# Converting doubles to floats on the chip: one DVE operation less per weight tile, and a parametric ReLU for the absolute value

## The chip, the core and the metric

The kernel runs on one core of a Trainium2 chip. Its time is device microseconds, from start to end of one execution. The engines are TensorE (PE), VectorE (DVE), ScalarE (ACT), GpSimd (POOL) and SyncE (SP), which here issues the transfers.

## The reference, cut to what matters

Three layers follow each other: an attention over a local window plus block summaries, a feed-forward layer with SoLU and a layer norm, and a feed-forward layer with ELU. Cut to the mathematics:

```python
B, H, S, D = 2, 8, 768, 64
k_sum, v_sum = blocks_of_32(k).max(), blocks_of_32(v).mean()
s = concat(where(|i - j| < 16, q @ k.T / 8, -1e9), q @ k_sum.T / 8 + log(32))
x = softmax(s) @ concat(v, v_sum)                      # 1536 tokens x 512

h = x @ w_in                                           # w_in 512 x 1024
z = h * softmax(h)
h = (z - mean(z)) / sqrt(var(z) + 1e-6) * g_ln @ w_out # w_out 1024 x 512

h = h @ w_in2                                          # w_in2 512 x 2048
out = where(h > 0, h, exp(h) - 1) @ w_out2             # w_out2 2048 x 512
```

The four weight matrices arrive as doubles (64-bit floats); q, k and v as 32-bit floats. Converting the weights to 32-bit floats is part of the kernel's work.

## The kernel before, in words

**Products.** The products with weights (h, y_ps, o_ps and c in the profile) run on PE in three matmuls each (`mm3x`, lines 105 to 107): both operands are split into a rounded high half and the rest, and high x high, high x low and low x high are added up. ACT writes a high half (`split`, L136; L147 where the weight is scaled by g_ln), DVE the low half (`lo_of`, L102; L148). The products of the attention run in plain 32-bit floats.

**Attention.** 24 steps of 64 queries, two per block of 128 tokens. For each step PE makes scores (s_ps, L216), DVE adds the mask and finds the minimum (L222), ACT takes exponentials (L225), DVE sums and inverts (L227, L228), POOL normalises (L230), PE transposes (p_ps, L235), ACT copies (pT, L237), and per two steps PE multiplies with v (x_ps, L252). The result becomes xT in a high half (ACT, L136) and a low half (DVE, L102).

**First layer.** 12 token blocks: h (PE), maximum (DVE, L277), exponential (ACT, L279), product (DVE, L280), sum of squares (ACT, L281), a few small operations, normalisation (POOL, L287), transposes (PE, L297) whose copies are lnT (ACT L299, DVE L102), then y_ps.

**Second layer.** First 512 tokens plain: h, ELU (L590 to L592), o_ps. The other 1024 tokens use a Strassen-like scheme on w_in2 (c in the profile). The converted w_out2 is stored to memory (w4d, L373) and fetched again (w4r, w4l, L402).

**Conversion of weights.** A tile of 128x512 doubles is loaded as pairs of 32-bit words (L114) into space that the results y (or bits) take later. `to_f32` then makes floats. Before, ACT takes the absolute value of the high word, read as a float (L123); POOL clamps it between two constants (L126); DVE shifts left by three and masks (L127); DVE takes the two top bits of the high word and ORs them in (L128); DVE shifts the low word right by 29 and ORs it in (L132). The 48 calls are 8 for w_in, 8 for w_out, 16 for w_in2 and 16 for w_out2. They share three buffers (conv) in turn. L127 of a tile waits on POOL, POOL on ACT, ACT on the load.

**Order.** A scheduler sets the order on PE, DVE, ACT and POOL from the operations' dependences and its own estimate of how long each takes; so a different operation moves others as well. SP's order is as written up to line 579, and PE's from line 650 on (the Strassen-like part). Conversions called with `pin` keep their place in the written order on ACT.

Of the kernel before, what the change touches and what calls it, by code (L numbers as in the profile page):

```python
# [9 lines left out]
F32 = mybir.dt.float32  # L10
# [4 lines left out]
AF = mybir.ActivationFunctionType  # L15
ALU = mybir.AluOpType
# [27 lines left out]
def f32_of(bits):  # L44
    return struct.unpack("f", struct.pack("I", bits))[0]

F64_TINY, F64_HUGE = f32_of(0x38000000), f32_of(0x47F00000)


@with_exitstack
def tile_kernel(ctx: ExitStack, tc: tile.TileContext, qd, kT, v, w_in, w_out, g_ln, w_in2, w_out2,
                ident_d, mask_d, avg_d, out):
    nc = tc.nc
    scale = 1.0 / math.sqrt(D)
# [60 lines left out]
    def to_f32(bits, outs=None, pin=False):  # L117
        words = bits.rearrange("p k (f two) -> p k f two", two=2)
        low, high = words[:, :, :, 0], words[:, :, :, 1]
        a = conv_t[:, state["conv"] % 3]  # L120
        state["conv"] += 1
        x = a.bitcast(F32)
        first = nc.scalar.activation(x, high.bitcast(F32), AF.Abs)  # L123
        if pin:
            tc.keep_in_program_order(first)
        nc.gpsimd.tensor_scalar(x, x, F64_HUGE, F64_TINY, op0=ALU.min, op1=ALU.max)  # L126
        nc.vector.tensor_scalar(a, a, 3, 0x3FFFFFF8, op0=ALU.logical_shift_left, op1=ALU.bitwise_and)  # L127
        nc.vector.scalar_tensor_tensor(a, high, -0x40000000, a, op0=ALU.bitwise_and, op1=ALU.bitwise_or)  # L128
        to = a if outs is None else outs
        if outs is not None:  # L130
            low, a = (t.rearrange("p (h k) f -> p h (k f)", h=2) for t in (low, a))
        nc.vector.scalar_tensor_tensor(to, low, 29, a, op0=ALU.logical_shift_right, op1=ALU.bitwise_or)  # L132
        return x
# [5 lines left out]
    def convert(bits, src, hi, lo, g=None, pin=False):  # L139
        if src is not None:  # L140
            load_words(bits, src)
        hi, lo = (t if len(t.shape) == 3 else t.rearrange("p (k f) -> p k f", k=KD) for t in (hi, lo))
        x = to_f32(bits, pin=pin)
        if g is None:
            split(hi, lo, x)
        else:
            nc.scalar.activation(hi, x, AF.Copy, scale=g)  # L147
            nc.vector.scalar_tensor_tensor(lo, x, g, hi.bitcast(F32), op0=ALU.mult, op1=ALU.subtract)  # L148
# [203 lines left out]
    def convert_w3(f, b):  # L352
        if f % 2 == 0:
            home(f // 2)
        to_f32(b, base_of(f).bitcast(I32), pin=True)
# [428 lines left out]
```

## Time and profile before

| | before |
|---|---|
| median of 3 runs (lowest to highest), us | 487.64 (487.32 to 488.69) |
| the profiled execution: its own time, us | 486.94 |
| the profiled execution: span, first to last instruction, us | 485.1 |
| mean granted TensorE clock | 0.995 |
| PE, DVE, ACT, POOL busy, us | 466.6, 332.4, 285.3, 125.7 |

The span is what the rows below are measured in; 1.8 us of the execution's own time lie around it. A busy share is an average over stages with different limits, and a busy PE is not a PE at its peak. What ended a wait is inferred from semaphores.

### The profile page before, as it was taken

Reading aid. Unit: us, or ns where it says so; the run is one execution under the profiler, and the core shown is the slowest. Engines: PE = TensorE matmul, PEld = TensorE weight load, DVE = VectorE, ACT = ScalarE, POOL = GpSimd, SP = SyncE. Lnnn points to the kernel's source line nnn. Section 1 sums busy time; section 2 is a strip of 40 time slices with the busy share of each in tenths; the row PEclk is TensorE's granted clock in tenths of the full one; section 3 lists DMA queues with packets and bytes.
Section 4 is the critical chain, followed back from the end, with each engine's and each line's share of the span. In section 5 each row is a group of like instructions: output and inputs, shape, how many; then the busy total and the mean of one; then the engine's idle time right before and its main releaser. Section 6 shows DMA issues by size and latency. Waiting matters only on the chain.

```text
span 485.1 us, 7476 instructions
## 1 busy us (share of the span) xinstructions
PE 466.6 (96%) x2600; PEld 391.0 (81%) x2600; DVE 332.4 (69%) x748; ACT 285.3 (59%) x623; POOL 125.7 (26%) x200
## 2 busy tenths in 40 slices
PE   7879999799999999999999999999999999999996
PEld 3566788689997998899888888888888888888885
DVE  3789868997688477979899999457575565550000
ACT  1776687995577347654964767467676666660001
POOL 2795376586544322313212200000000000000000
PEclk9989999999999999999999999999999999999999
DMA  8994997263253513397579752651212212388112
GB/s 276 356 363 144 291 276 226 84 201 109 82 167 107 153 55 117 101 336 264 180 255 334 277 208 98 214 177 45 84 47 86 86 45 87 104 300 290 45 43 86
DMA packets 40117, 82.47 MB, mean 170 GB/s; under 512 B 9616, under 2 KB 18448, under 8 KB 40080
## 3 DMA queue, kind: packets, MB, share of 16 engines
q1 hardware_dynamic: 40080, 82.00, 51.5%
q8 instruction: 20, 0.33, 0.3%
q14 instruction: 17, 0.14, 0.1%
HBM read 70.46 MB, written 11.53 MB: 169 GB/s over the span
## 4 chain that ended last, share of the span: by engine, by line
PE 80%; DVE 11%; DMA 4%; ACT 2%; issue 2%; POOL 0%; SPq 0%; DVEq 0%; POOLq 0%
PE o_ps L105 9%; PE o_ps L106 9%; PE o_ps L107 9%; PE h L107 6%; PE h L105 6%; PE h L106 6%; PE c L105 5%; PE c L106 5%; PE c L107 5%; PE y_ps L105 4%; PE y_ps L107 4%; PE y_ps L106 4%; DMA q_bd<-in_qd 3%; PE s_ps L216 2%; PE vs_ps L186 2%
## 5 line engine op out<-in xcount | busy, mean ns | idle before, releaser
L126 POOL TENSOR_SCALAR conv<-conv 128x512 f32<-128x512 f32 x48 | 37.4, 780 | 87.9 <-ACT conv L123 84.0
L230 POOL TENSOR_SCALAR sm<-sm,st 128x120 f32<-128x120 f32 x96 | 49.9, 537 | 29.9 <-DVE st L228 11.2
L105 PE MATMUL o_ps<-w4r,g_hl 128*128 128x512 f32 x128 | 49.8, 389 | 0.0
L106 PE MATMUL o_ps<-w4r,g_hl 128*128 128x512 f32 x128 | 49.8, 389 | 0.0
L107 PE MATMUL o_ps<-w4r,g_hl 128*128 128x512 f32 x128 | 45.3, 389 | 0.0
L105 PE MATMUL y_ps<-lnT,w_out 128*128 128x384 f32 x128 | 43.6, 341 | 1.0 <-DVE lnT L102 1.0
L105 PE MATMUL h<-w_in,xT 128*128 128x512 f32 x96 | 39.9, 418 | 3.4 <-ACT xT L136 3.3
L106 PE MATMUL y_ps<-lnT,w_out 128*128 128x384 f32 x128 | 43.2, 337 | 0.0
L107 PE MATMUL y_ps<-lnT,w_out 128*128 128x384 f32 x128 | 42.9, 337 | 0.0
L225 ACT ACTIVATE sm<-sm,st 128x120 f32<-128x120 f32 x96 | 36.7, 388 | 5.5 <-DVE st L222 3.8
L107 PE MATMUL h<-w_in,xT 128*128 128x512 f32 x96 | 39.1, 409 | 0.7 <-DVE xT L102 0.7
L106 PE MATMUL h<-w_in,xT 128*128 128x512 f32 x96 | 38.8, 406 | 0.0
L619 DVE COPY y<-o_ps 128x512 f32<-128x512 f32 x5 | 3.5, 690 | 42.9 <-PE o_ps L107 42.9
L591 ACT ACTIVATE y<-y 128x512 f32<-128x512 f32 x48 | 30.1, 630 | 0.8
L621 ACT ACTIVATE y<-o_ps 128x512 f32<-128x512 f32 x6 | 3.6, 599 | 43.9 <-PE o_ps L107 43.9
L123 ACT ACTIVATE conv<-y 128x512 f32<-128x512 f32 x30 | 20.1, 673 | 14.8 <-DMA y<-in_w_in 12.7
L216 PE MATMUL s_ps<-kw,q_bd 128*128 128x120 f32 x192 | 25.6, 276 | 2.6 <-DMA q_bd<-in_qd 1.7
L106 PEld LDWEIGHTS o_ps<-w4r,g_hl 128*128 128x128 f32 x128 | 24.1, 188 | 5.0
L107 PEld LDWEIGHTS o_ps<-w4r,g_hl 128*128 128x128 f32 x128 | 24.0, 188 | 5.0
L105 PEld LDWEIGHTS o_ps<-w4r,g_hl 128*128 128x128 f32 x128 | 24.0, 188 | 5.0
L216 PEld LDWEIGHTS s_ps<-kw,q_bd 128*128 128x128 f32 x192 | 24.0, 191 | 5.0 <-POOL kw L98 1.9
L102 DVE TENSOR_TENSOR g_hl<-y,g_hl 128x512 fp32r<-128x512 f32 x32 | 21.9, 685 | 8.6 <-ACT g_hl L136 8.5
(149 smaller groups left out, 1273.4 us busy)
## 6 DMA issues: line engine op xcount, KB each, us to landing
w4r<-w4d SPq DMA_DIRECT2D x38, 512.0 KB, 3.6
y<-in_w_in SPq DMA_DIRECT2D x16, 512.0 KB, 6.0
w4d<-w3f SPq DMA_DIRECT2D x16, 512.0 KB, 3.0
y<-in_w_out SPq DMA_DIRECT2D x14, 512.0 KB, 5.1
q_bd<-in_qd SPq DMA_DIRECT2D x24, 256.0 KB, 6.3
bits<-in_w_out SPq DMA_DIRECT2D x10, 512.0 KB, 5.4
w4l<-w4d SPq DMA_DIRECT2D x10, 512.0 KB, 4.9
vw<-in_v SPq DMA_DIRECT2D x24, 192.0 KB, 5.3
```

Source lines behind the costliest of these rows:

```text
L102: nc.vector.tensor_tensor(out_, x, hi.bitcast(F32), op=ALU.subtract)
L105: nc.tensor.matmul(ps, lhsT=l[0][ls], rhs=r[0][rs], start=first, stop=False, skip_group_check=parts)
L106: nc.tensor.matmul(ps, lhsT=l[0][ls], rhs=r[1][rs], start=False, stop=False, skip_group_check=parts)
L107: nc.tensor.matmul(ps, lhsT=l[1][ls], rhs=r[0][rs], start=False, stop=last, skip_group_check=parts)
L123: first = nc.scalar.activation(x, high.bitcast(F32), AF.Abs)
L126: nc.gpsimd.tensor_scalar(x, x, F64_HUGE, F64_TINY, op0=ALU.min, op1=ALU.max)
L186: nc.tensor.matmul(pst, lhsT=avg[:, c0:c0 + 128], rhs=vt, start=i == 0, stop=i == S // 128 - 1)
L216: nc.tensor.matmul(sps[:, p, 0:KW], lhsT=q_bd[n][:, p, :], rhs=kw[:, p, :], start=True, stop=True)
L225: nc.scalar.activation(sm[:, p, :], sm[:, p, :], AF.Exp, bias=nm[:, p:p + 1], scale=-1.0, accum_out=ss[:, p:p + 1])
L230: nc.gpsimd.tensor_scalar(sm[:, p, :], sm[:, p, :], ri[:, p:p + 1], 1.0, op0=ALU.mult, op1=ALU.mult)
L591: nc.scalar.activation(m, m, AF.Exp, scale=-1.0)
L621: nc.scalar.activation(o, ops[t], AF.Copy)
```

## The change

The high word of a double, read as a 32-bit float, has the double's sign, then the upper 8 of its 11 exponent bits as exponent, and 3 exponent bits and 20 bits of the fraction as fraction. The changed kernel multiplies this float by 2^-112 on ACT, by a parametric ReLU that multiplies negative values by another 2^32. After that a positive value has a float exponent from 0 to 31, a negative one from 32 to 63: the bit of value 32 is the sign. POOL clamps both sides, and one shift left by three on DVE drops the three top bits and puts sign, exponent and fraction where the 32-bit float has them. L128 of the old kernel falls away, and the mask of L127.

```diff
-F64_TINY, F64_HUGE = f32_of(0x38000000), f32_of(0x47F00000)
+TO_F32, SIGN_TO_28 = 2.0 ** -112, 2.0 ** 32
+MOST, LEAST = f32_of(0x0FF00000), f32_of(0x9FF00000)
...
-        first = nc.scalar.activation(x, high.bitcast(F32), AF.Abs)
+        first = nc.scalar.activation(x, high.bitcast(F32), AF.Prelu, scale=TO_F32, alpha=SIGN_TO_28)
         if pin:
             tc.keep_in_program_order(first)
-        nc.gpsimd.tensor_scalar(x, x, F64_HUGE, F64_TINY, op0=ALU.min, op1=ALU.max)
-        nc.vector.tensor_scalar(a, a, 3, 0x3FFFFFF8, op0=ALU.logical_shift_left, op1=ALU.bitwise_and)
-        nc.vector.scalar_tensor_tensor(a, high, -0x40000000, a, op0=ALU.bitwise_and, op1=ALU.bitwise_or)
+        nc.gpsimd.tensor_scalar(x, x, MOST, LEAST, op0=ALU.min, op1=ALU.max)
+        nc.vector.tensor_scalar(a, a, 3, None, op0=ALU.logical_shift_left)
```

In the changed file lines 50 to 127 of the old one stand one lower (105 to 107 are 106 to 108, L123 is L124, L127 is L128); from L132 on the numbers are the same. DVE issues 48 instructions less, the other engines as many as before, in an order that is partly new.

DVE at the first conversions, before (y is the loaded tile, conv the converted one, w_in_90 the low half of w_in):

```order
L127 TENSOR_SCALAR conv<-conv 128x512
L128 SCALAR_TENSOR_TENSOR conv<-y_65,conv 128x512
L132 SCALAR_TENSOR_TENSOR conv<-y_65,conv 128x512
L227 TENSOR_SCALAR st<-st 128x4
L228 RECIPROCAL st<-st 128x4
L102 TENSOR_TENSOR w_in_90<-conv,w_in_89 128x512
```

and now:

```order
L128 TENSOR_SCALAR conv<-conv 128x512
L132 SCALAR_TENSOR_TENSOR conv<-y_65,conv 128x512
L227 TENSOR_SCALAR st<-st 128x4
L228 RECIPROCAL st<-st 128x4
L103 TENSOR_TENSOR w_in_90<-conv,w_in_89 128x512
```

The two-input operation between shift and last step is gone; the rest stands as it did.

ACT ahead of the first xT, before (sm are softmax tiles, w_in_89 the high half of w_in):

```order
L123 ACTIVATE conv<-y_66 128x512
L225 ACTIVATE sm,st<-sm,st 128x120 x4
L136 ACTIVATE w_in_89<-conv 128x512
L225 ACTIVATE sm,st<-sm,st 128x120
L136 ACTIVATE xT<-x_ps 128x512
```

and now:

```order
L124 ACTIVATE conv<-y_66 128x512
L136 ACTIVATE w_in_89<-conv 128x512
L225 ACTIVATE sm,st<-sm,st 128x120 x5
L136 ACTIVATE xT<-x_ps 128x512
```

The rounding of w_in now stands ahead of the exponentials that it followed.

PE from the scores near 55 us of the old profile on, before (s_ps scores, x_ps product with v, p_ps transposes):

```order
L216 MATMUL s_ps<-kw_117,q_bd 128x120 x4
L252 MATMUL x_ps<-pT,vw_122 64x64 x8
L252 MATMUL x_ps<-pT,vw_121 64x64 x8
L235 MATMUL p_ps<-ident,sm 120x128 x4
L216 MATMUL s_ps<-kw_118,q_bd 128x120 x4
L235 MATMUL p_ps<-ident,sm 120x128 x4
L105 MATMUL h<-w_in_89,xT 128x512
L106 MATMUL h<-w_in_90,xT 128x512
L216 MATMUL s_ps<-kw_119,q_bd 128x120 x4
```

and now, with the same scores first:

```order
L216 MATMUL s_ps<-kw_117,q_bd 128x120 x4
L252 MATMUL x_ps<-pT,vw_122 64x64 x8
L252 MATMUL x_ps<-pT,vw_121 64x64 x8
L107 MATMUL h<-w_in_90,xT 128x512
L108 MATMUL h<-w_in_89,xT 128x512
L235 MATMUL p_ps<-ident,sm 120x128 x4
L216 MATMUL s_ps<-kw_118,q_bd 128x120 x4
L107 MATMUL h<-w_in_90,xT 128x512
L108 MATMUL h<-w_in_89,xT 128x512
L235 MATMUL p_ps<-ident,sm 120x128 x4
L216 MATMUL s_ps<-kw_119,q_bd 128x120 x4
L252 MATMUL x_ps<-pT,vw_124 64x64 x8
```

Before, eighteen h matmuls follow the last row shown, then the product with v and the transposes for the first scores; now eight more of the product with v (vw_123) follow, and those transposes directly.

## Rows read from the trace of the kernel before

**Rows 1.** The page: engine totals, busy us, share of the span, instructions.

```profile
PE 466.6 (96%) x2600; PEld 391.0 (81%) x2600; DVE 332.4 (69%) x748; ACT 285.3 (59%) x623; POOL 125.7 (26%) x200
```

**Rows 2.** PE's waits by releaser, whole span: us in total, times, longest.

```profile
PE h L105 <- ACT xT L136: 3.3, 2, 2.1
PE p_ps L235 <- POOL sm L230: 2.3, 3, 1.4
PE p_ps L235 <- DVE lnT L102: 1.2, 1, 1.2
PE y_ps L105 <- DVE lnT L102: 1.0, 1, 1.0
PE s_ps L216 <- ACT pT L237: 0.9, 1, 0.9
PE h L107 <- DVE xT L102: 0.7, 1, 0.7
```

**Rows 3.** Timeline of PE: start us, us, line, operation, [idle before].

```profile
54.59 0.39 PE L107 MATMUL h<-w_in,xT 128*128 128x512 f32 x1
54.81 1.05 PE L216 MATMUL s_ps<-kw,q_bd 128*128 128x120 f32 x8
55.79 1.15 PE L252 MATMUL x_ps<-pT,vw 120*64 120x64 f32 x32
56.87 0.65 PE L235 MATMUL p_ps<-ident,sm 128*120 128x128 f32 x4
...
91.08 0.62 PE L235 MATMUL p_ps<-ident,sm 128*120 128x128 f32 x4 [1.25 <-DVE lnT L102]
...
204.34 0.45 PE L105 MATMUL y_ps<-lnT,w_out 128*128 128x384 f32 x1 [1.03 <-DVE lnT L102]
```

**Rows 4.** Windows: busy us per engine (instructions), TensorE clock, DMA share, GB/s.

```profile
25.00:50.00 25.00, 21.20 (x139) 15.34 (x139) 22.01 (x74) 17.54 (x57) 17.69 (x29) 0.93 0.76 252
28.00:34.00 6.00, 5.07 (x20) 3.88 (x21) 3.83 (x8) 3.69 (x11) 5.82 (x10) 0.72 1.03 335
184.00:204.50 20.50, 19.46 (x117) 17.70 (x116) 19.62 (x38) 15.47 (x27) 6.44 (x7) 1.00 0.29 98
```

**Rows 5.** Operations that write conv: duration ns min/median/max, first and last start.

```profile
L126 POOL TENSOR_SCALAR conv<-conv x48: 608/620/2412, 13.8 to 277.5; 128x512 f32<-128x512 f32 x48
L127 DVE TENSOR_SCALAR conv<-conv x48: 391/417/848, 15.5 to 280.7; 128x512 int32<-128x512 int32 x48
L123 ACT ACTIVATE conv<-y x30: 652/672/702, 13.0 to 211.5; 128x512 f32<-128x512 f32 x30
L128 DVE SCALAR_TENSOR_TENSOR conv<-y,conv x30: 676/693/1501, 15.9 to 213.5; 128x512 int32<-128x512 int32 x30
```

**Rows 6.** Timeline of DVE, three of its L128 operations.

```profile
23.91 0.97 DVE L128 SCALAR_TENSOR_TENSOR conv<-y,conv 128x512 int32<-128x512 int32 x1
...
40.72 0.73 DVE L128 SCALAR_TENSOR_TENSOR conv<-y,conv 128x512 int32<-128x512 int32 x1
...
87.71 0.69 DVE L128 SCALAR_TENSOR_TENSOR conv<-y,conv 128x512 int32<-128x512 int32 x1
```

**Rows 7.** Timeline of POOL, normalising softmax tiles (L230).

```profile
28.11 3.09 POOL L230 TENSOR_SCALAR sm<-sm,st 128x120 f32<-128x120 f32 x4
...
33.01 1.40 POOL L230 TENSOR_SCALAR sm<-sm,st 128x120 f32<-128x120 f32 x4
...
43.40 2.54 POOL L230 TENSOR_SCALAR sm<-sm,st 128x120 f32<-128x120 f32 x4 [1.47 <-DVE st L228]
...
62.30 1.40 POOL L230 TENSOR_SCALAR sm<-sm,st 128x120 f32<-128x120 f32 x4 [0.56 <-DVE st L228]
```

**Rows 8.** Window of the L128 operations alone: DVE busy us (instructions).

```profile
180.00:210.00 30.00, 2.73 (x4) 1.00 0.36 117
```

**Rows 9.** Groups by line and shape, on ACT: busy us, mean ns, idle before.

```profile
L591 ACT ACTIVATE y<-y 128x512 f32<-128x512 f32 x48 | 30.1, 630 | 0.8
L123 ACT ACT_TABLE_LOAD x1 | 1.3, 1283 | 0.7 <-PEq L776 0.7
```

## The prediction

> **What bounds the kernel now.** First the line of engine totals: TensorE (PE) is busy 96% of the span, VectorE (DVE) 69%, ScalarE (ACT) 59%, GpSimd (POOL) 26% [rows 1]. So a change that takes work from DVE alone can win only what PE loses by waiting. Second, PE's waits by releaser: the six groups that end on ACT, POOL or DVE add up to 3.3 + 2.3 + 1.2 + 1.0 + 0.9 + 0.7 = 9.4 us [rows 2], and the last of them ends at 204.34 us [rows 3]. Behind that, PE's own work sets the end, and what DVE saves there buys nothing. Third, the windows: from 25 to 50 us DVE is busy 22.01 of 25 us while PE has 3.8 us free; from 28 to 34 us the granted clock is 0.72, a mixture of the two levels 1.2 and 2.4 GHz, after PE had waited for its operands [rows 4]. At full clock these 6 us would be worth 0.28 x 6 = 1.7 us less. Waits and clock together bound any gain at 9.4 + 1.7 = 11.1 us.
>
> The profiled execution took 486.94 us, 0.70 under the median of the runs shown (487.64, from 487.32 to 488.69). The sum is made against 486.94 and then carried over to the median. About 0.3%, 1.5 us, is what a measurement of this kernel can tell from no change.
>
> **The change part by part.**
> *Removed:* one two-input DVE operation (L128) from each of 48 conversions. The 30 in the row have a median of 0.69 us [rows 5]; 48 x 0.69 = 33 us of DVE time. What of it lies on PE's path is taken place by place:
>
> (a) 26 to 30 us. PE waits 2.1 us for ACT's high half of xT and then 0.7 us for DVE's low half [rows 2]. An L128 of 0.97 us at 23.91 stands in DVE's queue ahead of the softmax pieces and the converted weights that ACT works off before that high half [rows 6]. The new order on ACT puts the rounding of these weights (L136) ahead of four exponentials that it stood behind, so ACT now waits for the conversion first, and the high half gains little, by estimate 0.2 us. The low half comes 0.97 us earlier in DVE's own queue, less about 0.3 us in which DVE then waits for ACT. I take 0.65 us for both waits together; bounds 0 and 2.8.
>
> (b) 45 to 46 us. POOL waited 1.47 us for DVE's reciprocal before it normalised four tiles from 43.40 [rows 7]; an L128 of 0.73 us at 40.72 is in that DVE queue [rows 6]. PE's two shorter waits on POOL are here, 2.3 - 1.4 = 0.9 us [rows 2]. I take 0.7; bounds 0 and 0.9.
>
> (c) 91 to 95 us. PE waits 1.25 us for DVE's half of lnT [rows 3], and right behind it 1.4 us on POOL [rows 2]; DVE's queue has an L128 of 0.69 us at 87.71 [rows 6]. The whole row moves up once, so 0.7; bounds 0 and 2.65.
>
> (d) 203 us. PE waits 1.03 us on DVE's lnT [rows 3]. DVE is busy 19.62 of the 20.5 us ahead [rows 4], and four L128 lie there, 2.73 us [rows 8]: more than the wait, so all of it goes, 1.0; bounds 0 and 1.03.
>
> The other waits (0.9 us for ACT's pT, 3.3 - 2.1 = 1.2 of those for ACT's xT) have no conversion just ahead of them: 0, at best 2.1.
>
> *Altered:* the first DVE operation (L127) loses its mask and keeps 128x512 integers in and out. No row shows a shift alone; its nearest bounds are 0.391, the quickest with the mask, and 0.69, that of the two-input operation. I take its own median, 0.417 [rows 5], since size, type and number of tensors stay. ACT's Abs becomes a parametric ReLU, 48 times. No row shows that function; the nearest bound it by 0.630, an exponential of this size [rows 9], and by 1.34, twice the Abs (a second pass). I take 0.672 as before [rows 5], for Abs and exponential, two different functions, are 0.04 us apart. POOL's clamp only has other constants: 0.620 as before, bounds its own 0.608 and 2.412 [rows 5].
>
> *Moved:* no instruction leaves its engine, but the order on each is made anew. SP's transfers are the same; where their order differs is the stage that fetches w_in2 and w_out2 and stores the converted w_out2. There PE waits for no transfer now: past 204.34 us no wait of PE is listed [rows 2, 3]. So 0, with a wait of PE for w4r as what would refute it. The 33 us of DVE time give weights earlier in that stage, but PE takes them no earlier: 0.
>
> Sum: 0.65 + 0.7 + 0.7 + 1.0 = 3.05 us; 486.94 - 3.05 = 483.89, on the median **484.6 us**.
>
> **The port of DVE and POOL.** Four normalisations of POOL took 3.09 us from 28.11 us, beside a full DVE queue, and 1.40 us from 33.01 [rows 7]. So DVE's operations also cost POOL time, which (b) and (c) leave out, because two other two-input operations stay in every conversion and would fall on the same POOL work. The Trainium skill, page "SBUF — State Buffer", section "SBUF: two separate sides", says that a DVE operation with two SBUF inputs and a GpSimd operation that reads SBUF exclude each other for a whole instruction; the trace agrees (3.09 against 1.40). If that rule decided, both of PE's waits on POOL would go whole, 0.2 us more in (b) and 1.4 more in (c): a sum of 4.65, or 483.0 us.
>
> **The rivals.**
> *More comes back.* Waits chain, and a PE that stalls less keeps its clock. For: the clock of 0.72 and POOL's 3.09 - 1.40 = 1.69 us [rows 4, 7]. Against: each place has a second releaser (ACT in (a), POOL in (c)). With (a) to (d) gone whole (2.8 + 0.9 + 2.65 + 1.0 = 7.35) and half of the clock's 1.7, it is 8.2 us, 479.4 us; with all 11.1 us, 476.5.
>
> *Hidden.* The releasers behind DVE take over: ACT in (a), whose work the change does not shorten, POOL in (b) and (c). Only (d) is won: 486.6 us. For: the longest wait ends on ACT, and 2.3 us on POOL [rows 2]. Against: both wait on DVE there.
>
> *Slower, by PE's new row.* Near 55 us PE issues scores (L216), and its transposes of the softmax of these very scores (L235) come with two more blocks of scores and twenty h matmuls in between. In the new order there are only four h matmuls between them. PE's own work from the one to the other is then 0.98 + 1.08 + 0.65 + 0.98 + 0.65 + 0.98 + 1.08 us, by the distances of starts and the whole duration of the transposes, and 4 x 0.22 for h [rows 3]: 7.3 us. The softmax of these scores took from 54.81 [rows 3] to the end of POOL's work at 63.70 [rows 7], 8.9 us. PE's queue is in order, so what a round takes over 7.3 us becomes a wait: 1.6 us. With three such rounds (the new order packs the stretch of (c) as tightly) it is 4.8 us, in place of the 0.9 for pT, and (c)'s 0.7 is lost: 3.05 - 0.7 - 3.9 = -1.55, or 489.2. It decides from rounds of about 8.9 us on, three times. Against: by then DVE has some six L128, 4 us, less behind it.
>
> *The function costs a table.* If the parametric ReLU lay in another table than the exponential, each of the 48 conversions, which stand among exponentials on ACT, would add two loads of 1.28 us [rows 9]: 123 us of ACT. ACT is free for 41% of the span [rows 1], so most is hidden; a tenth at the end gives 500 us. Against: the changed program holds one load, as the old one. A ReLU that is only slow, 1.34 us, adds 48 x 0.67 = 32 us; a tenth, 3.2 us, would cancel the sum. The Trainium skill, page "ScalarE: Activation LUTs", section "What ACT_TABLE_LOAD costs", gives a switch as 1283 ns and a drain, 2.66 us; the trace's one load agrees with the first figure, no run shows the second. By it the tenth would be 26 us, 513 us.
>
> **How the numbers follow.** The forecast (1.5 to 5 us won) 0.50, with a range of its own of 482.6 to 486.1 us; more comes back 0.11; hidden (within 1.5 us either way) 0.21; slower by PE's row 0.15; by the function 0.03. Faster than 486.2 is then 0.61, the same 0.21, slower than 489.1 0.18. The range goes down most of the way to 479.4, to 480.5, and up past the three rounds and a part of a fourth, to 489.9. Below it lie some 0.07, above it some 0.10.
>
> **What would show it.** Right: DVE's busy time falls from 332 to about 299 us; 48 activations of 0.67 us; one table load; shorter waits of PE for the first xT, none on lnT near 203 us, and none behind it. Wrong in size: PE's waits for POOL's sm grow between 50 and 65 us, or new ones appear near 90 us. Wrong altogether: activations over 0.8 us, more than one table load, or PE waiting for w4r or g_hl past 204 us, where every edit is costed at nothing.

## The result, and the profile after

The changed kernel takes **480.62 us** (median of 5 runs, 480.08 to 481.47); the kernel before took 487.37 in the same comparison (5 runs, 486.57 to 488.69). The ratio is 0.9858, 95% interval 0.9839 to 0.9877: 6.7 us faster. The forecast was 484.6, with 3.05 us won. The direction was right; the gain is more than twice the forecast, below the own range of the likeliest case (482.6 to 486.1) and 0.1 us inside the whole range (480.5 to 489.9).

The profiled execution took 480.23 us, its span is 478.4. The rows below are its own; line numbers from 102 to 127 are one higher than before, and the shift is L128 now. First the page: engine totals, and the clock in 40 slices of the span.

```profile
PE 463.1 (97%) x2600; PEld 389.8 (81%) x2600; DVE 302.1 (63%) x700; ACT 282.8 (59%) x623; POOL 117.5 (25%) x200
...
PEclk9999999999999999999999999999999999999999
```

DVE has lost 30.3 us of its 332.4 [rows 1], by the 48 operations that are gone; the forecast had 33. The operations that write conv (duration in ns min/median/max, first and last start):

```profile
L127 POOL TENSOR_SCALAR conv<-conv x48: 612/617/3030, 13.3 to 265.0; 128x512 f32<-128x512 f32 x48
L128 DVE TENSOR_SCALAR conv<-conv x48: 396/420/1075, 15.1 to 268.3; 128x512 int32<-128x512 int32 x48
L124 ACT ACTIVATE conv<-y x30: 650/668/697, 12.6 to 203.3; 128x512 f32<-128x512 f32 x30
```

Against [rows 5] no median here has moved by more than 0.004 us: the parametric ReLU takes 0.668 us where the Abs took 0.672, the shift without its mask 0.420 for 0.417, the clamp 0.617 for 0.620. PE's waits by releaser (us in total, times, longest):

```profile
PE s_ps L216 <- DMA q_bd<-in_qd: 2.8, 2, 1.8
PE h L106 <- ACT xT L136: 2.1, 3, 1.1
PE vs_ps L186 <- DMA v_sb<-in_v: 1.5, 1, 1.5
PE busy L465 <- DVE ln L462: 1.2, 1, 1.2
PE p_ps L235 <- DVE st L222: 1.0, 1, 1.0
PE y_ps L106 <- ACT y L314: 0.9, 1, 0.9
PE h L108 <- DVE xT L103: 0.8, 2, 0.5
PE vs_ps L186 <- DVE st L222: 0.6, 1, 0.6
PE p_ps L235 <- POOL sm L230: 0.3, 1, 0.3
PE x_ps L252 <- ACT pT L237: 0.2, 1, 0.2
```

Of the six groups of [rows 2], the one on POOL fell from 2.3 to 0.3 us and that on ACT's xT from 3.3 to 2.1; the longest wait for xT is no longer 2.1 but 1.1, one near 146 us that stood in the kernel before as well (1.12 us, at 152.09). The timeline of PE (start us, us, line, operation, idle before) at the places that the prediction named:

```profile
26.53 0.50 PE L106 MATMUL h<-w_in,xT 128*128 128x512 f32 x1 [0.83 <-ACT xT L136]
...
27.58 0.50 PE L108 MATMUL h<-w_in,xT 128*128 128x512 f32 x1 [0.32 <-DVE xT L103]
27.92 0.40 PE L106 MATMUL h<-w_in,xT 128*128 128x512 f32 x1
28.15 0.40 PE L107 MATMUL h<-w_in,xT 128*128 128x512 f32 x1
...
33.39 1.96 PE L186 MATMUL vs_ps<-v_sb,avg 128*128 128x512 f32 x4 [0.57 <-DVE st L222]
...
45.66 0.50 PE L108 MATMUL h<-w_in,xT 128*128 128x512 f32 x1 [0.46 <-DVE xT L103]
...
56.80 1.15 PE L252 MATMUL x_ps<-pT,vw 120*64 120x64 f32 x32 [0.18 <-ACT pT L237]
...
85.85 0.65 PE L235 MATMUL p_ps<-ident,sm 128*120 128x128 f32 x4 [1.00 <-DVE st L222]
...
197.60 0.45 PE L106 MATMUL y_ps<-lnT,w_out 128*128 128x384 f32 x1 [0.91 <-ACT y L314]
```

The first two waits were 2.15 and 0.75 us and are 0.83 and 0.32. Behind them the h products start 0.23 us apart. And the window that stood at a clock of 0.72 [rows 4] (busy us by engine, then the granted clock, DMA share, GB/s) is at full clock:

```profile
28.00:34.00 6.00, 5.43 (x36) 4.41 (x35) 4.51 (x25) 5.12 (x16) 5.50 (x11) 1.00 1.04 339
```

Three things may have given the 6.7 us: DVE's time (theory 1), the new order of the instructions (theory 2), or what the clock made of the shorter waits. A cheaper function (theory 3) and POOL's port (theory 4) are the other rivals.

### The profile page after: what moved, and what is told of

Read it like the earlier page. It is cut to its first block, busy times and chain, and to the rows that moved or that the text cites. A ratio compares the mean times of both kernels' runs of the same rounds, so it can differ in the third digit from the quotient of the medians.

```text
span 478.4 us, 7421 instructions
## 1 busy us (share of the span) xinstructions
PE 463.1 (97%) x2600; PEld 389.8 (81%) x2600; DVE 302.1 (63%) x700; ACT 282.8 (59%) x623; POOL 117.5 (25%) x200
## 4 chain that ended last, share of the span: by engine, by line
PE 86%; DMA 6%; DVE 4%; ACT 2%; issue 1%; SPq 0%
PE o_ps L108 9%; PE o_ps L107 9%; PE o_ps L106 9%; PE h L108 8%; PE h L106 8%; PE h L107 7%; PE c L108 5%; PE c L107 5%; PE c L106 5%; PE y_ps L106 4%; PE y_ps L108 4%; PE y_ps L107 4%; DMA y<-in_w_in 4%; PE s_ps L216 2%; DMA k_sb<-in_kT 2%; PE x_ps L252 2%
## 5 line engine op out<-in xcount | busy, mean ns | idle before, releaser
L127 POOL TENSOR_SCALAR conv<-conv 128x512 f32<-128x512 f32 x48 | 37.2, 775 | 83.5 <-ACT conv L124 79.7
L230 POOL TENSOR_SCALAR sm<-sm,st 128x120 f32<-128x120 f32 x96 | 44.5, 481 | 27.4 <-DVE st L228 12.9
L106 PE MATMUL h<-w_in,xT 128*128 128x512 f32 x96 | 39.3, 411 | 2.1 <-ACT xT L136 2.1
L108 PE MATMUL h<-w_in,xT 128*128 128x512 f32 x96 | 38.4, 400 | 0.8 <-DVE xT L103 0.8
L107 PE MATMUL h<-w_in,xT 128*128 128x512 f32 x96 | 38.5, 401 | 0.0
L124 ACT ACTIVATE conv<-y 128x512 f32<-128x512 f32 x30 | 20.0, 671 | 18.0 <-DMA y<-in_w_in 11.7
L222 DVE CUSTOM_DVE_ANT_0 sm<-s_ps,mask 128x120 f32<-128x120 f32 x96 | 21.5, 276 | 13.1 <-PE s_ps L216 13.1
L107 PEld LDWEIGHTS o_ps<-w4r,g_hl 128*128 128x128 f32 x128 | 24.1, 188 | 5.0
L106 PEld LDWEIGHTS o_ps<-w4r,g_hl 128*128 128x128 f32 x128 | 24.0, 188 | 5.0
```

Of the source, the lines that this page charges most:

```text
L106: nc.tensor.matmul(ps, lhsT=l[0][ls], rhs=r[0][rs], start=first, stop=False, skip_group_check=parts)
L107: nc.tensor.matmul(ps, lhsT=l[0][ls], rhs=r[1][rs], start=False, stop=False, skip_group_check=parts)
L108: nc.tensor.matmul(ps, lhsT=l[1][ls], rhs=r[0][rs], start=False, stop=last, skip_group_check=parts)
L124: first = nc.scalar.activation(x, high.bitcast(F32), AF.Prelu, scale=TO_F32, alpha=SIGN_TO_28)
L127: nc.gpsimd.tensor_scalar(x, x, MOST, LEAST, op0=ALU.min, op1=ALU.max)
L222: nc.vector.tensor_tensor_reduce(sm[:, p, :], sps[:, p, 0:KW], mask[:, mi, :], -scale, 3.0e38, op0=ALU.add, op1=ALU.min, accum_out=nm[:, p ...
```

## The experiments

Two means serve in most of them. The first keeps the order: each engine's instructions (PE, ACT, DVE, POOL) are chained by ordering-only dependencies in the order that another kernel has, so that operations and order can be exchanged apart:

```
+    for engine, runs in ORDER.items():
...
+        for x, y in zip(order, order[1:]):
+            tc.add_manual_dep(y, x.name, mybir.DependencyInfo(
+                mybir.DependencyClass.NoSync, mybir.DependencyReason.DATA), reason="order")
```

The second is a two-input DVE operation that changes nothing, in the place of the one removed:

```
         nc.vector.tensor_scalar(a, a, 3, None, op0=ALU.logical_shift_left)
+        nc.vector.scalar_tensor_tensor(a, high, 0, a, op0=ALU.bitwise_and, op1=ALU.bitwise_or)
```

Every ratio is to the kernel before, run beside it (medians of 487.06 to 487.38 us), with its 95% interval.

**The function alone.** The change, with that operation kept:

> The changed conversion with a two-input operation of the same shape kept on DVE behind the shift (it combines the high word and 0 with the result and changes nothing). All engines then stand in the order of before. The parametric ReLU, the shift without its mask and the clamp's new constants are all that is left of the change. Theory 1 and theory 2 both expect 487.4 us within 1.0: the function is worth nothing by itself. Theory 3, that the shift without a mask, or POOL's clamp, is what became cheaper: 482 or less.

487.53 us, ratio 1.0007 (0.9986 to 1.0028). The parametric ReLU, the bare shift and the clamp's constants are worth nothing by themselves, for good or ill, to within a microsecond; the rival of a table or a slow function falls here too.

**New operations in the old order, and the old operations in the new.**

> The changed conversion (no two-input operation, parametric ReLU), but PE, ACT, POOL and DVE pinned to the order that they had before. Theory 1, the DVE time itself is what was won: 480.6 us, within 1.0. Theory 2, the new order of PE, ACT and DVE won it: 487.4, within 1.0. If both share it, in between: then the distance to 480.6 is what the order is worth. By the prediction's own step (a), where the new order on ACT took most of the gain away, the old order with the shorter DVE queue would be faster still than the change: 479 to 480.

483.66 us (481.47 to 484.82), ratio 0.9916 (0.9886 to 0.9946): in between, so DVE's time by itself wins part. The old order is slower than the change, not faster, as the prediction's step (a) would have had it.

> The kernel before with all its operations (Abs, mask, the two-input operation), but PE, ACT, POOL and DVE pinned to the order of the change, the two-input operation right behind its shift. Theory 1 (DVE time): 487.4 us within 1.0, or slower, since DVE has the old work in an order made for less. Theory 2 (order): 480.6 within 1.0.

499.58 us, ratio 1.0246 (1.0217 to 1.0276): 12 us slower than before. Theory 2 is out; theory 1 had allowed for "slower", without a figure. So neither theory holds alone. Without the shorter DVE queue the new order costs 12 us; with it, it is worth another 3.0 over the old order (480.62 against 483.66, intervals apart). Put the other way, the operation is worth 3.7 us in the old order and 19 in the new. That an order made for a short DVE queue packs its work closer is my reading and not shown by itself. PE's waits in the second kernel show where the old operations then come late:

```profile
PE o_ps L107 <- DVE g_hl L102: 2.4, 5, 0.7
PE h L107 <- DVE xT L102: 2.1, 3, 1.4
...
PE y_ps L105 <- DVE st L222: 1.7, 1, 1.7
...
PE p_ps L235 <- DVE st L222: 0.9, 1, 0.9
PE p_ps L235 <- POOL sm L230: 0.4, 1, 0.4
```

The 2.4 us on g_hl lie past 205 us, where neither the kernel before nor the change waits.

**Is it PE's order?** New operations, PE in the new order, ACT, DVE and POOL in the old:

> New operations, PE in the order of the change, but ACT, DVE and POOL in the order of before. The order was worth 3.0 us between x1_new_ops_old_order and the change. If it is PE's order (other blocks between scores and the transposes of their softmax, so no wait for pT near 57 us): 480.6 to 481.5. If PE's order needs those of ACT and DVE: as x1_new_ops_old_order, 483.7, or slower.

501.50 us, ratio 1.0301 (1.0275 to 1.0327). PE's order is worth nothing without the order of those that feed it; the four belong together, and which engine's part brings how much can't be told from this.

**Which conversions.** In the old order, the operation left out only of w_in's 8 conversions, or only of the other 40:

```
+        if state["conv"] > 8:
+            nc.vector.scalar_tensor_tensor(a, high, 0, a, op0=ALU.bitwise_and, op1=ALU.bitwise_or)
```

> In the order of before, the two-input operation left out of the first 8 conversions (w_in) alone. The trace of x1_new_ops_old_order was 3.85 us ahead of before at 62 us and 5.22 at the end. If the 8 make what is won until then, the trace ends 3.8 us ahead and the median gains three quarters of the 3.7 of x1_new_ops_old_order: 484.6 us, within 1.0. If every conversion counts alike, 8 of 48: 486.8.

485.28 us, ratio 0.9936 (0.9911 to 0.9962): 2.1 us by the medians, 1.9 to 4.3 by the interval.

> In the order of before, the two-input operation kept in the 8 conversions of w_in and left out of the other 40: the counterpart of winold_new_only_w_in_old_order, which won 2.1 us. All 48 in this order won 3.7. If the two parts add up: 1.6 us, 485.8. If the clock's drops near 30 us, which then stay, hide or repeat them: 486.5 to 487.4.

485.63 us, ratio 0.9973 (0.9953 to 0.9993): 1.4 us by the medians, 0.3 to 2.3 by the interval. Together 3.5, and both at once gave 3.7: as far as such intervals can tell, they add up. By the medians a sixth of the removed operations, those of the first 50 us, makes over half of this gain. The same 8 in the new order:

> The two-input operation is left out of the first 8 conversions only (those of w_in, all before 50 us) and kept in the other 40; PE, ACT and POOL pinned to the order of the change, DVE too. Theory 1 with the gain made by 62 us (the lag between the two traces is 4.8 us there): 482.6 us within 1.0. If the gain were spread over all 48 conversions, 8 of them would give 1.1 us: 486.3.

495.88 us, ratio 1.0178 (1.0144 to 1.0212). A miss: both expectations left out that the new order with the old operations in it costs 12 us. Against those 499.58 the 8 conversions give 3.7 us.

**The clock.** Is the clock of 0.72 at 28 to 34 us made by PE's wait for xT? The kernel before, with 8 products of zeros while PE waits there (no wait gets shorter):

```
-            hs[j] = psh.tile([128, F1], F32, tag="h", name="h")
+            hs[j] = psh.tile([128, F1], F32, tag="h", name="h"); fill(j)
...
+    def fill(j):
+        for i in range(8 if j == 0 else 0):
+            nc.tensor.matmul(hs[j][:, 0:512], lhsT=zero[:, 0:128], rhs=zero, start=True, stop=True)
```

> The kernel before, in its own order, with 8 products of zeros (bf16, 128x512, as those at the start) put into the bank of the first h, right ahead of its first product, where PE idles 2.15 us for xT. They shorten no wait. If the clock between 28 and 34 us falls because of that idle time, the granted clock there goes from 0.72 to 1.0 and the h products stand 0.23 apart and not 0.43: 1.4 to 1.7 us less, 485.8 us. If the clock falls for another reason, 487.4.

486.24 us, ratio 0.9968 (0.9945 to 0.9990): 1.1 us faster by the medians, 0.5 to 2.7 by the interval, by products that compute nothing. Timeline of PE and two windows of this kernel:

```profile
26.06 1.67 PE L110 MATMUL h<-ln 128*128 128x512 bf16 x7 [0.16 <-issue]
27.93 0.50 PE L105 MATMUL h<-w_in,xT 128*128 128x512 f32 x1 [0.19 <-ACT xT L136]
```

```profile
28.00:34.00 6.00, 5.26 (x31) 4.13 (x32) 5.23 (x18) 4.55 (x15) 5.82 (x9) 1.00 1.04 339
44.00:50.00 6.00, 5.35 (x23) 4.53 (x24) 6.00 (x23) 3.73 (x12) 2.24 (x5) 0.72 1.02 287
```

The clock holds at 28 us, and in this run falls near 45 us instead, where PE waits for POOL's sm (0.61, 0.48 and 0.44 us): less than the full 1.7 comes back. Five of its twelve runs had a mean clock of 0.998 or over, of the 29 of the kernel before beside it four. The reverse, the change with the wait made long again:

```
+        for i in range(2 if j == 0 else 0):
+            nc.scalar.activation(xT[j][0], xps, AF.Copy)
         split(*xT[j], xps)
```

> The change in its own order, but ACT rounds the first xT three times over (the same operation, 128x512 from PSUM), so that PE's wait for it grows by about 1.2 us, from 0.83 to about the 2.15 that stood there before. No time of DVE changes. If the idle time brings the clock down, the granted clock from 28 to 34 us falls to about 0.72 as it was before, and the time is 1.2 + 1.7 = 2.9 us longer: 483.5 us. If the clock has another cause: 1.2 us at most, 481.8, with the clock at 1.0.

482.83 us, ratio 0.9909 (0.9885 to 0.9932). Its timeline of PE and the window:

```profile
28.37 0.50 PE L106 MATMUL h<-w_in,xT 128*128 128x512 f32 x1 [2.12 <-ACT xT L136]
...
29.98 0.63 PE L107 MATMUL h<-w_in,xT 128*128 128x512 f32 x1
30.41 0.63 PE L108 MATMUL h<-w_in,xT 128*128 128x512 f32 x1
```

```profile
28.00:34.00 6.00, 5.63 (x23) 4.37 (x24) 2.65 (x8) 3.85 (x12) 4.33 (x10) 0.72 1.04 339
```

PE idles 2.12 us, the h products go from 0.23 to 0.43 us apart, and the window reads 0.72, as before. Four of its six runs had a mean granted clock of 0.994 to 0.996 and took 482.64 to 483.71 us; two had 0.998 and 0.999 and took 481.43 and 481.54. So the wait alone costs some 0.9 us against 480.62, about as much as the change's own runs differ, and the runs with the lower clock take 1.1 to 2.3 more. The idle time sets the clock off, though not in every run.

The runs of the kernel before sort the same way. Of 29, four had a mean clock of 0.998 or over and took 485.35 to 485.92 us; sixteen had 0.995 or 0.996 and took 486.17 to 488.00; nine had 0.988 to 0.990 and took 489.02 to 490.35. All five of the change had 0.998 or over.

**How much of the order is clock?** Fillers in the new operations' old order, and two more profiled runs of that kernel itself:

> New operations in the old order, as in x1_new_ops_old_order (median 483.66, from 481.47 to 484.82, its profiled run the fastest, with the clock at 1.0 from 28 to 34 us), with 4 products of zeros ahead of the first h. If the other runs of that kernel are slower because their clock fell there, the median comes down to its fastest, 481.5 us, and the order is worth about 1 us of the change's 6.7. If its runs differ for another reason, 483.7 as it was, and the order is worth 3.

482.49 us, ratio 0.9888 (0.9853 to 0.9923). The interval overlaps that without fillers, so by times this is unclear; five of its six runs had a mean clock of 0.998 or over, where without fillers it was one of six. One run with a clock of 1.0 took 483.64 all the same, so the clock is not all that differs between runs.

> The same kernel as x1_new_ops_old_order, looked at again. If the 1.7 us between its profiled run (481.47) and most of its others are the clock, a run near 483.5 shows one stretch of some 3.4 us at half clock, the h products in it 0.43 apart, right behind PE's waits for xT near 27 us or those near 88 us. If the run is near 483.5 and the clock is at 1.0 throughout, it is something else, transfers for instance.

> As x1look_a, once more: of two looks at least one should be of a run with the lower mean clock, which five of six runs had. Expected 483.5 with one stretch at half clock, or 481.5 with none.

483.84 and 483.68 us, each with one stretch at half clock, in different places. The windows, of the first and then of the second:

```profile
58.00:62.00 4.00, 4.00 (x15) 3.47 (x16) 2.30 (x18) 4.00 (x18) 2.97 (x8) 0.57 1.07 311
```

```profile
28.00:32.00 4.00, 3.25 (x10) 2.49 (x10) 2.41 (x6) 2.88 (x7) 3.82 (x8) 0.57 1.04 328
```

0.43 of 4 us is 1.7 us each time. In the second the h products slow down right behind the two waits for xT, 1.31 and 0.75 us; in the first behind PE's waits of 0.35 and 0.87 us from 55 to 58 us:

```profile
57.83 1.73 PE L216 MATMUL s_ps<-kw,q_bd 128*128 128x120 f32 x8 [0.87 <-ACT pT L237]
```

The first profiled run of this kernel had waits of 1.10 and 0.62 us for xT, no such stretch, and took 481.47.

**The port.** A DVE operation with one SBUF input in the same place:

```
+        turned = a.rearrange("p k f -> p f k")
+        nc.vector.tensor_scalar(turned, turned, 0, None, op0=ALU.bitwise_or)
```

> New operations in the old order, with a DVE operation of one SBUF input (128x512, strided, in place, it changes no bit) where the two-input operation was. DVE then stays about as busy as before while what it may take from POOL by its second input is gone. Theory 1, DVE's time decides: 487.4 us within 1.0 if the new operation takes about 0.69 us. Theory 4, the second input decides, by making POOL wait: 483.7 as x1_new_ops_old_order, and POOL's normalisations near 28 us shorter.

487.60 us, ratio 1.0002 (0.9977 to 1.0028). Its engine totals and its group on conv; then the third of the four tiles that POOL normalises near 28 us, in the kernel before beside an L128 (DVE, from 29.52 us), here beside the operation with one input (from 29.64), and in the old order without any such operation:

```profile
PE 469.4 (96%) x2600; PEld 393.4 (81%) x2600; DVE 333.1 (68%) x748; ACT 285.2 (58%) x623; POOL 138.5 (28%) x200
...
L130 DVE TENSOR_SCALAR conv<-conv x48: 728/759/1534, 16.1 to 285.8; 128x512 int32<-128x512 int32 x48
```

```profile
29.48 0.87 POOL L230 TENSOR_SCALAR sm<-sm,st 128x120 f32<-128x120 f32 x1
...
29.59 0.93 POOL L232 TENSOR_SCALAR sm<-sm,st 128x120 f32<-128x120 f32 x1
...
28.42 0.36 POOL L230 TENSOR_SCALAR sm<-sm,st 128x120 f32<-128x120 f32 x1
```

The operation is 0.07 us longer than the one it stands for, which is a weakness of this run. POOL's tile takes 0.93 us beside an operation with one input, 0.87 beside one with two, and 0.36 beside neither: an operation of DVE there holds POOL up, and no second input is needed for it. So theory 4 falls as it was put. But the run did not take POOL's delay away, as it was meant to: POOL is busy 138.5 us in it and 125.7 before [rows 1]. It leaves open how much of the gain is DVE's own time and how much is POOL's delay. It does show that pinning costs nothing by itself: all four engines are held to the old order, and the time is that of the kernel before.

**One operation more.** The change, with the low word's bits left out in 32 conversions (the lowest three bits of those weights stay zero):

```
-        nc.vector.scalar_tensor_tensor(to, low, 29, a, op0=ALU.logical_shift_right, op1=ALU.bitwise_or)
+        if outs is not None:
+            nc.vector.scalar_tensor_tensor(to, low, 29, a, op0=ALU.logical_shift_right, op1=ALU.bitwise_or)
```

> The change, with the second two-input operation (the low word's bits) left out too in the 32 conversions that write no other tile, so their lowest three bits stay zero; another 32 x 0.69 = 22 us less on DVE, in an order made anew. If DVE still sets PE's waits: 5.9 us of waits on ACT, DVE and POOL are left and a part like the first goes, 1.5 to 3 us: 478.5 us. If the other releasers (ACT's rounding, transfers) now end last: 480.6 within 0.7. If the new order costs more than it brings: over 481.3.

479.68 us, ratio 0.9847 (0.9823 to 0.9872): 0.9 us under the change, with overlapping intervals, so unclear, and less than I expected. DVE is busy 282.2 us there, and the longest waits of PE are for transfers (q_bd), and then for ACT's xT:

```profile
PE s_ps L217 <- DMA q_bd<-in_qd: 3.6, 3, 2.1
PE h L106 <- ACT xT L137: 2.6, 2, 1.3
```

The first 30 us taken from DVE bought 6.7 us, the next 20 about 0.9, and by the intervals anything from nothing to some 2.

## Why the prediction was too small

The whole can now be laid out as a ladder of profiled executions. Before, 486.94, with one stretch at half clock. New operations in the old order, also with one such stretch: 483.84 and 483.68, so 3.2 us for DVE's time. The same without the stretch: 481.47, one run and the fastest of six, so 2.3 us, of which the windows give 1.7 to the clock. The change, in its own order: 480.23, so 1.2 us. Sum 6.7. A single run of this kernel may differ by a microsecond for other reasons, so the steps are good to about that. Of the 3.0 us between the medians of the two orders it puts 1.2 on the order as such, and the rest on the clock, which fell in five of six runs in the old order and in none of five in the new.

All runs together, sorted by their mean clock, agree. At 0.993 to 0.996 the kernel before has a median of 487.35 us (12 of the 17 runs beside the old-order kernel), the new operations in the old order 483.95 (five runs): 3.4 us for DVE's time at a like clock. At 0.998 or over the kernel before took 485.26 to 485.92 us (nine runs beside three sets of kernels), which is 1.2 to 2.0 under the median of its comparison. The change is still 4.6 to 5.3 us faster than those runs, so the clock has no more than some 2 of the 6.7 us.

PE's waits at five places, in us, by the timelines:

| | before | new operations, old order | the change |
|---|---|---|---|
| (a) xT, 26 to 30 us | 2.15 + 0.75 | 1.10 + 0.62 | 0.83 + 0.32 |
| (b) near 45 us | 0.42 + 0.49 | none | 0.46, and 0.57 at 33 us |
| st and then pT, 54 to 61 us | 0.34 + 0.88 | 0.25 + 0.87 | 0.18 |
| (c) 85 to 95 us | 1.25 + 1.41 | 0.55 + 0.41 + 0.53 | 1.00 + 0.25 + 0.16 |
| (d) near 200 us | 1.03 | 0.98 | 0.91 |
| sum | 8.72 | 5.31 | 4.68 |

- **The step that failed first is the clock, set to 0** (bound 1.7). It was read from the right row [rows 4], and the prediction even said what it came from, PE's wait for its operands, but then shortened that wait and left the clock out of its sum. In the change the window of 28 to 34 us reads 1.00 in place of 0.72, so the 1.7 us came whole, and its five runs keep the mean clock at 0.998 or over. The filled and the stalled kernel show the cause from both sides.
- **The second is "moved order 0", and in (a) the claim that the new order on ACT takes the gain away.** ACT's half of xT did not gain 0.2 us but 1.32 in the wait (2.15 to 0.83), of which 1.05 came in the old order already: ACT is itself held by DVE. Ahead of that xT it waits for DVE's softmax pieces (L222), 1.53 us in the kernel before and 0.63 in the old order with the new operations; in the change it does wait for the conversion first, as the prediction has it, for 0.96 us, and is done earlier all the same (the high half of xT starts at 27.55, 26.61 and 25.91 us). In this order:

```profile
25.12 0.40 ACT L225 ACTIVATE sm<-sm,st 128x120 f32<-128x120 f32 x1 [1.53 <-DVE st L222]
...
24.18 0.39 ACT L225 ACTIVATE sm<-sm,st 128x120 f32<-128x120 f32 x1 [0.63 <-DVE st L222]
...
23.45 0.63 ACT L136 ACTIVATE w_in<-conv 128x512 fp32r<-128x512 f32 x1 [0.96 <-DVE conv L132]
```

  The prediction named that queue and then took ACT for a releaser of its own. The wait for pT, also set to 0, is 0.87 in the old order still and gone in the new alone, but for 0.18 us ahead of another product. The other wait for ACT's xT, set to 0 too, did stay: 1.12 us in all three.
- (b) was 0.7 for both waits on sm; in the old order all 0.91 went. In the new order it is given back by two other waits on DVE, 0.46 and 0.57.
- (c) was 0.7; it is 1.2 us in either order. (a), (b) and (c) were taken too small by 0.5, 0.2 and 0.5 (in the old order: 1.2, 0.9 and 1.2).
- **(d) was 1.0 and is 0.1.** Here the reading was wrong in kind. DVE's 19.62 busy us of 20.5 [rows 4] do not make it late. The timelines of PE, ACT and DVE in the old order with the new operations:

```profile
197.09 1.03 PE L297 MATMUL t_ps<-ident,ln 128*128 128x128 f32 x8
...
197.73 0.60 ACT L299 ACTIVATE lnT<-t_ps 128x512 fp32r<-128x512 f32 x1
...
198.36 0.69 DVE L103 TENSOR_TENSOR lnT<-t_ps,lnT 128x512 fp32r<-128x512 f32 x1 [1.03 <-ACT lnT L299]
...
199.10 0.44 PE L106 MATMUL y_ps<-lnT,w_out 128*128 128x384 f32 x1 [0.98 <-DVE lnT L103]
```

  It is a round from PE over ACT and DVE back to PE. DVE had idled 1.03 us and began as soon as ACT was done; a shorter queue can't shorten the round. In the kernel before, ACT was done at 203.52 us and DVE began at 203.61: 0.09 us was all there was to win. In the change's own order DVE is not the last at this place: PE waits 0.91 us for ACT's copy of y (L314), which stands behind both copies lnT.
- So the 3.05 us of (a) to (d) agree with the 3.2 measured for DVE's time by itself, but partly by luck: (d)'s 0.9 too much stands against 1.2 too little in the others.
- *Past 204 us nothing* was right: the change's trace lists no wait of PE for w4r or g_hl there. *Altered* was right in all three operations.
- The rivals. "More comes back" is what happened, by its own first half (a PE that stalls less keeps its clock), though (d) did not come back, and its figure counted only half of the clock. "Hidden" falls: 483.66 even in the old order. "Slower by PE's new row" falls for the change, where the wait that was to grow, on sm, is 0.3 us; and even with the old operations in the new order, 12 us slower, PE waits only 0.9 us for st and 0.4 for sm ahead of its transposes, not the 4.8 that it set for three rounds. That the order can turn against the kernel was right; where it would was not. "A table" falls.
- The port. A second input is not needed to hold POOL up near 28 us (its tile took 0.93 us beside one input, 0.87 beside two). The Trainium skill, page "SBUF — State Buffer", section "SBUF: two separate sides", ties the exclusion to a DVE operation with two SBUF inputs or in a 2-port performance mode; no run here shows which mode the operation with one input ran in, so its delay of POOL neither bears the page out nor refutes it. The waits on POOL did go almost whole, as the sum of 4.65 had it. What brought that differs by place. POOL's tiles in the old order with the new operations, at (b) and at (c), and then in the kernel before at (c):

```profile
39.91 2.07 POOL L230 TENSOR_SCALAR sm<-sm,st 128x120 f32<-128x120 f32 x4 [1.47 <-DVE st L228]
...
89.06 1.79 POOL L230 TENSOR_SCALAR sm<-sm,st 128x120 f32<-128x120 f32 x4 [1.36 <-DVE st L228]
...
94.02 1.80 POOL L230 TENSOR_SCALAR sm<-sm,st 128x120 f32<-128x120 f32 x4 [2.00 <-DVE st L228]
```

  At (c) POOL works as long as before and only starts earlier, behind DVE: that is DVE's time. At (b) it takes 2.07 us for 2.54 [rows 7], so up to 0.5 us there may be POOL's delay.
- One slip in the reading: the six groups of [rows 2] are not all that end on DVE. The trace of the kernel before has two more, 1.2 us at the very start, which the change has too, and 0.3 us on st near 58 us, which is gone in the change. The bound of 11.1 us was short by that 0.3.

Of the 6.7 us, the waits in the table give 4.0 and the clock 1.7; 1.0 us is not tied to a single wait. Some 0.3 of it lies ahead of the first place: PE's scores for which q_bd lands last start at 22.38 us before and at 22.12 in the change, though PE's waits for q_bd add up to 1.7 us before and 2.8 now.

## What to carry to other kernels

Where a window shows a lowered clock behind a wait, price the wait and the clock together: an edit that shortens the wait may win both. Ask of each releaser whether it waits for the engine that you relieve (ACT did), and of each wait whether the releaser was late because of its queue or because its own input came late: a high busy share tells neither. Where a scheduler decides, an operation less is also a new order; pinning the order separates the two, and the new order can be worth as much as 3 us with the edit and cost 12 without it.

## Not expected of the hardware

Eight products of zeros in a wait made the unchanged kernel 1.1 us faster (0.9945 to 0.9990), and held the clock there. Runs of the kernel before go by their mean granted clock, from 485.4 to 485.9 us at 0.998 or over up to 489.0 to 490.4 at the lowest; and in profiles of kernels that differ little the stretch at half clock lies at 28, 45 or 58 us. Ahead of it stood one wait of PE of 2.1 us, or waits of 1.31 and 0.75, of 0.35 and 0.87, or of 0.61, 0.48 and 0.44 us; but a run with waits of 1.10 and 0.62 us had no such stretch, so these runs give no length of wait that decides. An integer operation in place on 128x512 with one input took 0.759 us when its elements were read strided, and 0.420 in the shift that reads them in a row.
